# A planned kernel changes its PSUM layout: two double-bank and four single-bank tiles in place of four double-bank ones, scores chunk by chunk, and a planner that holds tiles back

## The chip, the cores and the metric

The kernel runs on one core of one Trainium2 chip. The metric is the device time of one execution in microseconds (us). Five engines take part, each working through its own list of instructions in order: PE (TensorE, matrix products and transposes; its weight loads are listed as PEld), DVE (VectorE), ACT (ScalarE), POOL (GpSimd) and SP, which issues nearly all DMAs. They wait for each other through semaphores.

## What is computed

A linear-attention recurrence (4 batches, 8 heads, 768 tokens, 48 values a head), whose output goes into a mixing block (384 channels):

```
state = 0                                        # per batch, head: D x D
for t in range(S):
    y[t] = r[t] @ (state + outer(u * k[t], v[t]))
    state = w[:, None] * state + outer(k[t], v[t])
x = y of all heads side by side                  # B, S, 384
theta = x @ w_theta
yr = w_tok_r @ (x * cos(theta));  yi = w_tok_i @ (x * sin(theta))
u = x + yr + yi
out = u + relu(u @ w_ch)
```

## The kernel before, in words

The 768 tokens of a batch are six chunks of 128, worked on as three pairs of chunks. There are so twelve pairs, and the names below are those of the steps and of the tiles that the profile prints.

For each batch, POOL scales r by powers of w (`Rw`, L491; on DVE in batch 0), PE transposes it in four groups (L472) and ACT copies the result out of PSUM (`RT`, L260). For each pair (`attention`):

- POOL scales k (`Kw`, L519), PE transposes it (L472, 8 transposes), ACT or DVE copies it out (`KT`, L260 or L262), and ACT casts v (`vb`, L260).
- PE makes the scores (16 matmuls on 64 rows, L543: two chunks, four pairs of heads, two heads each), DVE multiplies them by the mask (`mAT`, L549, two instructions). DVE makes `PD` (L554) and PE the diagonal term from it (L562), which ACT or DVE copies (`dg`) and POOL spreads over v (`yd`, L569).
- PE accumulates the outer products of k and v onto the state (L594, L586); DVE takes the state out after the first chunk (`Sb`, L601) and, scaled, after the second (`Sb`, L607).
- PE makes the pair's output from state and masked scores (L621, L626), DVE adds `yd` and has `x` (L633). PE transposes `x` (L472; copied out to `xT`) and multiplies by w_theta (L645); ACT takes sine and cosine (L649, L652), DVE and POOL the products `zr` (L655) and `zi` (L658).

When all three pairs of a batch have `zr` and `zi`, `mixing` makes the token product of each chunk in four parts of three matmuls that accumulate in one bank (L677), DVE adds `x` (`un`, L683), PE transposes (L472; `uT`), multiplies by w_ch (L694), DVE finishes (`fin`, L698) and SP stores (L702). The token weights come in twelve pieces that PE transposes first (L455, "W flips" here), from the same ring of ten `ld` buffers that k and v are loaded into.

Nothing of this order is written out by hand. Every step is a task with a cost, a priority, the keys that it reads and writes, and the PSUM space that it acquires and uses. `Plan.order` plays these tasks through with those costs: at each moment each engine takes the ready task of lowest priority number whose PSUM space is free, and the instructions are recorded in this order. On the chip each engine then runs its list in order, whatever the real durations are. The layer that records the instructions adds the semaphore waits; it keeps track of PSUM accesses by tile.

PSUM has eight banks. Before, they are four tiles of two banks. A task that needs one bank takes half a tile, so that two tasks that have nothing to do with each other can hold the two halves:

```
P = Plan(8)
banks = [ps.tile([C, 2, 512], F32, name=f"bank{i}") for i in range(4)]

def bank(tok):
    i = P.bank_of[tok]
    return banks[i // 2][:, i % 2]
```

Transposes, outer products, the diagonal term and the token product take one bank. The output of a pair, theta, the product with w_ch and a W flip take two. The scores of a pair take two times two: for each head of a pair of heads (`hi`) a double tile with both chunks.

Of the kernel before, what the change touches and what calls it, by code (L numbers as in the profile page):

```python
# [21 lines left out]
ENGINES = (PE, DVE, ACT, POOL, SP)  # L22


class Task:
    __slots__ = ("opts", "fn", "deps", "prio", "seq", "acq", "uses", "nwait", "users", "ready",
                 "start", "end", "mode", "lock", "eng", "name")


class Plan:  # L30
# [7 lines left out]
    def __init__(self, nbanks):  # L38
        self.tasks, self.writer, self.readers = [], {}, {}
        self.nbanks = nbanks  # L40
        self.bank_uses, self.bank_of, self.width = {}, {}, {}
# [30 lines left out]
    def pick_banks(self, acq, free, now):  # L72

        got = {}
        avail = [i for i in range(self.nbanks) if free[i] <= now]
        for tok in sorted(acq, key=lambda k: -self.width[k]):
            if self.width[tok] == 2:
                c = [i for i in avail if i % 2 == 0 and i + 1 in avail]
                if not c:
                    return None  # L80
                i = min(c, key=lambda i: max(free[i], free[i + 1]))
                avail.remove(i)
                avail.remove(i + 1)
            else:
                if not avail:
                    return None
                i = min(avail, key=lambda i: ((i ^ 1) in avail, free[i]))
                avail.remove(i)
            got[tok] = i
        return got  # L90

    def order(self):
        for t in self.tasks:
            t.users, t.nwait, t.ready = [], len(t.deps), 0.0
# [14 lines left out]
        free = [0.0] * self.nbanks  # L109
# [4 lines left out]
        while len(out) < n:  # L114
            for e in ENGINES:
                while free_at[e] <= now:
                    best, got = None, None
                    for t in waiting[e]:
                        if t.ready > now or (t.lock and port > now):
                            continue  # L120
                        if best is not None and (t.prio, t.seq) >= (best.prio, best.seq):
                            continue
                        if len(t.opts) > 1:
                            mine = now + t.opts[e][0]
                            if any(max(free_at[o], now) + t.opts[o][0] < mine
                                   for o in t.opts if o != e):
                                continue
                        g = {}
                        if t.acq:
                            g = self.pick_banks(t.acq, free, now)  # L130
                            if g is None:
                                continue
                        best, got = t, g
                    if best is None:
# [4 lines left out]
                    for tok, i in got.items():  # L139
                        self.bank_of[tok] = i  # L140
                        for j in range(self.width[tok]):
                            free[i + j] = INF
# [8 lines left out]
                    free_at[e] = now + ns  # L151
                    t.end = now + ns + lat
                    out.append(t)
                    for b in t.uses:
                        left[b] -= 1
                        freed[b] = max(freed.get(b, 0.0), t.end)
                        if left[b] == 0:
                            for j in range(self.width[b]):
                                free[self.bank_of[b] + j] = freed[b]
                    for x in t.users:  # L160
                        x.ready = max(x.ready, t.end)
# [4 lines left out]
            nxt += [t.ready for e in ENGINES for t in waiting[e] if t.ready > now]  # L166
# [59 lines left out]
def build(ctx, tc, nc, r, k, v, w, u, moe_w_theta, moe_w_tok_r, moe_w_tok_i, moe_w_ch, out):  # L226
# [12 lines left out]
    P = Plan(8)  # L239
    banks = [ps.tile([C, 2, 512], F32, name=f"bank{i}") for i in range(4)]  # L240

    def dbl(tok):
        return banks[P.bank_of[tok] // 2]

    def bank(tok):
        i = P.bank_of[tok]
        return banks[i // 2][:, i % 2]

    def bank16(tok):
        i = P.bank_of[tok]  # L250
        return banks[i // 2].bitcast(BF16)[:, i % 2]
# [57 lines left out]
    def setup():  # L309
# [6 lines left out]
        def fills(e):  # L316
# [7 lines left out]
        P.add({DVE: (600, 100)}, fills, wr=["ones", "wu", "pi2", "uw", "bmask"], prio=-200)  # L324
# [161 lines left out]
    def heads(b, base):  # L486

        rf, Rw, RT = r_fs[b % NR], Rws[0], RTs[b % 2]
        for hp in range(HP):
# [5 lines left out]
            opts = {POOL: pool_op(576, 2.1)}  # L495
# [9 lines left out]
    def attention(b, pr, base):  # L505
# [16 lines left out]
        opts = {POOL: pool_op(2 * HD)}  # L522
# [12 lines left out]
        tk = [("A", g, hi) for hi in range(2)]  # L535

        def scores(e):
            for c in range(2):
                cc = 2 * pr + c
                for hp in range(HP):  # L540
                    for hi in range(2):
                        q = slice(hi * Dp, (hi + 1) * Dp)
                        nc.tensor.matmul(dbl(tk[hi])[:, c, hp * C:(hp + 1) * C],  # L543
                                         KT[q, c, hp, :], RT[q, hp, cc * C:(cc + 1) * C],
                                         start=(hp == 0), stop=(hp == HP - 1))
        P.add({PE: pe_op(470)}, scores, rd=[kT] + rt_keys, acq=[(t, 2) for t in tk],
              prio=pb + 2, mode=1, name="scores")
        for hi in range(2):
            P.add({DVE: dve_op(8 * C)}, lambda e, hi=hi: nc.vector.tensor_mul(  # L549
                mAT[:, hi].rearrange("p a h t -> p (a h) t"),  # L550
                dbl(tk[hi]).rearrange("p a (h t) -> p (a h) t", h=HP), bc(mask01, 1, 2 * HP)),
                use=[tk[hi]], rd=["mask"], wr=[kM + (hi,)], prio=pb + 3, name="mask")
# [39 lines left out]
        def outer0(e):  # L592
# [8 lines left out]
        P.add({DVE: dve_op(HD)}, lambda e: nc.vector.tensor_mul(  # L601
            Sb_mid, bank(tS)[:, :HD].rearrange("p (h e) -> p h e", h=HP), bc(bmask, 1, HP)),
            use=[tS], rd=["bmask"], wr=[S_mid], prio=pb + 2.2, name="S")
# [9 lines left out]
        def outputs(e):  # L613
            for c in range(2):
# [10 lines left out]
                for h in range(H):  # L625
                    nc.tensor.matmul(dbl(ty)[:, c, h * D:(h + 1) * D], mAT[:, h % 2, c, h // 2, :],  # L626
# [131 lines left out]
```

## Time and profile before

| what | value |
|---|---|
| times of the runs shown | 235.33, 173.79 and 174.2 us, median 174.2 us |
| the profiled execution's own time | 173.87 us |
| its span, first to last instruction | 172.2 us |
| PE busy | 137.9 us (80%) |
| DVE busy | 113.2 us (66%) |
| POOL busy | 76.2 us (44%) |
| ACT busy | 71.6 us (42%) |

All durations come from the profiled execution, whose time is 1.7 us longer than its span. In rows of the timeline the columns are the start in us from the span's start, the duration in us, engine, line, operation, output and inputs by the program's names, and in brackets how long the engine stood idle just before, with what ended that. Rows of several instructions carry a count (x6). A busy PE is not PE at its peak, since matmuls are pipelined: one of 128x384 shows 326 ns, while 24 of them in a row take 3.90 us. In rows of the waits, the columns are the engine and line that waited, what it waited for, the total in us, the number of times and the longest.

### The profile page before, as it was taken

How to read it: one execution, taken by the hardware profiler on the slowest of the kernel's cores; microseconds unless marked ns; L12 is line 12 of the kernel's file. 1: busy time of each engine (PE TensorE's matmuls, PEld its weight loads, DVE VectorE, ACT ScalarE, POOL GpSimd, SP SyncE). 2: the span in 40 equal slices, each digit the busy share in tenths (PEclk: the TensorE clock that was granted, in tenths of full speed). 3: DMA queues.
4: the chain of work that ended last, by engine and by line, in shares of the span. 5: the costliest groups of instructions: out<-in, count | busy, mean ns of one | idle time of the engine just before them, and what ended most of it. 6: DMA issues, size and time to landing. Idle time of an engine off the chain costs nothing.

```text
span 172.2 us, 3640 instructions
## 1 busy us (share of the span) xinstructions
PE 137.9 (80%) x1491; PEld 96.1 (56%) x1491; DVE 113.2 (66%) x163; ACT 71.6 (42%) x102; POOL 76.2 (44%) x62
## 2 busy tenths in 40 slices
PE   3056699997969869968699999997899999699970
PEld 1046568786745646646485657566656665455530
DVE  6274976963418897476888668646799885344361
ACT  3966236775953425457633532556105213000000
POOL 6003328079941507999799791330333332100000
PEclk9999999999999999999969999999999999999995
DMA  5999999999993399799999900220020022020222
GB/s 164 239 240 163 169 372 373 392 372 157 177 159 53 92 325 152 136 197 195 344 161 157 168 12 20 75 91 0 4 91 4 0 93 89 6 91 0 91 91 91
DMA packets 59962, 25.00 MB, mean 145 GB/s; under 512 B 50473, under 2 KB 58410, under 8 KB 59946
## 3 DMA queue, kind: packets, MB, share of 16 engines
q1 hardware_dynamic: 59920, 24.78, 65.7%
q8 instruction: 11, 0.18, 0.5%
q14 instruction: 5, 0.04, 0.1%
q10 hardware_dynamic: 26, 0.00, 0.0%
HBM read 20.06 MB, written 4.72 MB: 144 GB/s over the span
## 4 chain that ended last, share of the span: by engine, by line
PE 53%; DVE 21%; ACT 11%; issue 7%; DMA 3%; POOL 3%; ACTq 1%; DVEq 0%; POOLq 0%
PE bank L677 22%; PE bank L472 8%; PE bank L694 7%; PE bank L645 6%; DVE mAT L549 5%; ACT RT L260 5%; DVE un L683 3%; DMA wu<-in_u_dram 3%; PE bank L626 2%; DVE fin L698 2%; DVE uT L262 2%; POOL zi L658 2%; PE bank L543 2%; DVE xT L262 2%; DVE Sb L601 2%
## 5 line engine op out<-in xcount | busy, mean ns | idle before, releaser
L677 PE MATMUL bank<-zi,WiT 128*128 128x384 bf16 x144 | 29.9, 326 | 3.7 <-DVE Sb L607 1.4
L569 POOL TENSOR_TENSOR yd<-dg,vb 128x768 bf16<-128x768 f32 x12 | 17.6, 1473 | 33.1 <-ACT dg L260 33.1
L677 PE MATMUL bank<-zr,WrT 128*128 128x384 bf16 x144 | 29.6, 326 | 2.9 <-ACT RT L260 1.4
L658 POOL TENSOR_TENSOR zi<-x,sin 128x768 bf16<-128x768 bf16 x12 | 19.9, 1657 | 25.0 <-ACT sin L649 25.0
L549 DVE TENSOR_TENSOR mAT<-bank,mask 128x1024 bf16<-128x1024 f32 x24 | 29.0, 1216 | 1.0 <-PE bank L543 1.0
L519 POOL TENSOR_TENSOR Kw<-ld,wpinv 128x768 bf16<-128x768 f32 x11 | 19.8, 1822 | 11.7 <-ACT RT L260 11.7
L683 DVE TENSOR_TENSOR un<-bank,x 128x384 bf16<-128x384 f32 x24 | 13.2, 555 | 16.4 <-PE bank L677 9.4
L677 PEld LDWEIGHTS <-WiT 128*128 128x128 bf16 x144 | 13.3, 97 | 11.7 <-issue 4.6
L677 PEld LDWEIGHTS <-WrT 128*128 128x128 bf16 x144 | 13.1, 97 | 11.1 <-issue 4.2
L649 ACT ACTIVATE sin<-bank 128x768 bf16<-128x768 f32 x12 | 9.7, 811 | 20.5 <-DVE fin L698 10.6
L260 ACT ACTIVATE RT<-bank 128x768 bf16<-128x768 bf16 x16 | 12.8, 815 | 9.4 <-PE bank L472 5.5
L491 POOL TENSOR_TENSOR Rw<-r_f,wpow 128x576 bf16<-128x576 f32 x12 | 16.6, 1409 | 0.0
L698 DVE SCALAR_TENSOR_TENSOR fin<-bank,un 128x768 f32<-128x768 f32 x12 | 11.5, 956 | 6.5 <-PE bank L694 6.4
L645 PE MATMUL bank<-Wth,xT 128*128 128x384 bf16 x72 | 14.7, 343 | 1.2 <-DVE xT L262 0.9
L694 PE MATMUL bank<-Wch,uT 128*128 128x384 bf16 x72 | 13.7, 327 | 1.4 <-DVE uT L262 1.4
L633 DVE TENSOR_TENSOR x<-bank,yd 128x768 bf16<-128x768 f32 x12 | 11.4, 951 | 2.5 <-PE bank L626 1.3
L655 DVE TENSOR_TENSOR zr<-bank,x 128x768 bf16<-128x768 f32 x12 | 11.4, 950 | 1.1 <-ACT bank L652 1.1
L472 PE MATMUL bank<-ident,Rw 128*128 128x128 bf16 x96 | 8.9, 241 | 3.4 <-ACT RT L260 1.9
L260 ACT ACTIVATE vb<-ld 128x768 bf16<-128x768 f32 x12 | 10.1, 840 | 3.5 <-DMA ld<-in_v_dram 3.4
L260 ACT ACTIVATE KT<-bank 128x1024 bf16<-128x1024 bf16 x7 | 7.2, 1023 | 9.5 <-PE bank L677 4.0
L626 PE MATMUL bank<-vb,mAT 128*128 128x48 bf16 x192 | 9.6, 189 | 1.7 <-DVE mAT L549 1.6
L652 ACT ACTIVATE bank<-bank,pi 128x768 f32<-128x768 f32 x12 | 10.5, 875 | 0.0
(76 smaller groups left out, 212.3 us busy)
## 6 DMA issues: line engine op xcount, KB each, us to landing
ld<-in_k_dram SPq DMA_DIRECT2D x24, 192.0 KB, 5.3
ld<-in_v_dram SPq DMA_DIRECT2D x24, 192.0 KB, 5.2
out_dram<-fin SPq DMA_DIRECT2D x12, 384.0 KB, 2.5
r_f<-in_r_dram SPq DMA_DIRECT2D x3, 1152.0 KB, 7.8
ld<-in_moe_w_tok_r_dram SPq DMA_DIRECT2D x6, 384.0 KB, 8.6
ld<-in_moe_w_tok_i_dram SPq DMA_DIRECT2D x6, 384.0 KB, 8.2
r_f<-in_r_dram SPq DMA_DIRECT2D x2, 576.0 KB, 4.6
ld<-in_moe_w_theta_dram SPq DMA_DIRECT2D x1, 384.0 KB, 5.0
```

Source lines behind the costliest of these rows:

```text
L260: nc.scalar.activation(dst, src, Act.Copy)
L472: nc.tensor.matmul(bank16(tok)[:, i * C:(i + 1) * C], s, ident, is_transpose=True, start=(i == 0), stop=(i == n - 1))
L491: eng_of[e].tensor_mul(Rw[:, :, 2 * hp:2 * hp + 2, :D].transpose([0, 2, 1, 3]), rf[:, 2 * hp:2 * hp + 2, :].rearrange("p h (n d) -> p h n ...
L519: eng_of[e].tensor_mul(Kw[:, :, :, :D].rearrange("p a h d -> p (a h) d"), Ls[ik][:, :, :, :D].rearrange("p a h d -> p (a h) d"), wpinv.rea ...
L549: P.add({DVE: dve_op(8 * C)}, lambda e, hi=hi: nc.vector.tensor_mul(mAT[:, hi].rearrange("p a h t -> p (a h) t"), dbl(tk[hi]).rearrange("p ...
L569: P.add({POOL: pool_op(2 * HD, 1.7)}, lambda e: nc.gpsimd.tensor_mul(yd.rearrange("p a (h d) -> p (a h) d", h=H), wide(dg, D), vb.rearrang ...
L645: nc.tensor.matmul(dbl(th)[:, t, :HD], xT[:, ND * t + dk, :], Wth[:, dk, :], start=(dk == 0), stop=(dk == ND - 1))
L658: P.add({POOL: pool_op(2 * HD, 1.9)}, lambda e: nc.gpsimd.tensor_mul(zi[:, 2 * pr:2 * pr + 2], x[:, 2 * pr:2 * pr + 2], sn), rd=xk + [("si ...
L677: nc.tensor.matmul(bank(tm)[:, :HD], WT[:, so, to * C:(to + 1) * C], z[:, so], start=(part == 0 and j == 0), stop=(part == 3 and j == 2))
L683: P.add({DVE: dve_op(HD)}, lambda e, tm=tm, t=t, to=to: nc.vector.tensor_add(un[:, t], bank(tm)[:, :HD], x[:, to]), use=[tm], rd=[("x", zj ...
L694: nc.tensor.matmul(dbl(tf)[:, t, :HD], uT[:, ND * t + dk, :], Wch[:, dk, :], start=(dk == 0), stop=(dk == ND - 1))
L698: P.add({DVE: dve_op(2 * HD)}, lambda e: nc.vector.scalar_tensor_tensor(fin, dbl(tf)[:, :, :HD], 0.0, un, op0=Alu.max, op1=Alu.add), use=[ ...
```

## The change

Three things are changed together.

PSUM becomes six tiles: two of two banks (slots 0 and 1) and four of one bank (slots 2 to 5). A task that needs one bank takes the smallest free tile that holds it, so a single-bank task may hold a double tile, but no two tasks share one.

The scores of a pair become two tasks, one for each chunk, each with 8 matmuls into one double tile (the two halves are now the two heads) and one mask instruction. `mAT` is turned round accordingly.

The planner changes in five points. A task that finds no tile free keeps the one that will be free first from tasks of higher priority number (`kept`). Readiness is counted for each engine, so that a task on the same engine as the one before it doesn't wait out the latency. PE costs count 1.6 times in the first 25 us (`cold`). POOL's costs for k and r are a little higher. And the state after the first chunk may be taken out by ACT too, in two copies of 64 partitions (the four `Sb` tiles are cleared once at the start, by four DVE fills).

```
+SLOTS = (2, 2, 1, 1, 1, 1)
...
+            c = [i for i in avail if self.slots[i] >= self.width[tok]]
+            if not c:
+                return None
+            i = min(c, key=lambda i: (self.slots[i], free[i]))
...
                             if g is None:
+                                c = [i for i in range(len(self.slots)) if i not in kept and
+                                     self.slots[i] >= max(self.width[k] for k in t.acq)]
+                                if c:
+                                    kept.add(min(c, key=lambda i: free[i]))
                                 continue
...
+                        if now < self.cold:
+                            ns *= 1.6
...
+                            x.ready[o] = max(x.ready[o], t.done if o == e else t.end)
...
-    P = Plan(8)
-    banks = [ps.tile([C, 2, 512], F32, name=f"bank{i}") for i in range(4)]
+    P = Plan(SLOTS)
+    banks = [ps.tile([C, n, 512], F32, name=f"bank{i}") for i, n in enumerate(SLOTS)]
...
+            for t in Sbs:
+                nc.vector.memset(t, 0.0)
...
-            opts = {POOL: pool_op(576, 2.1)}
+            opts = {POOL: pool_op(576, 2.15)}
...
-        opts = {POOL: pool_op(2 * HD)}
+        opts = {POOL: pool_op(2 * HD, 2.15)}
...
-        tk = [("A", g, hi) for hi in range(2)]
-
-        def scores(e):
-            for c in range(2):
-                cc = 2 * pr + c
+        for c in range(2):
+            tk, cc = ("A", g, c), 2 * pr + c
+
+            def scores(e, tk=tk, c=c, cc=cc):
...
-                        nc.tensor.matmul(dbl(tk[hi])[:, c, hp * C:(hp + 1) * C],
+                        nc.tensor.matmul(dbl(tk)[:, hi, hp * C:(hp + 1) * C],
...
-        P.add({PE: pe_op(470)}, scores, rd=[kT] + rt_keys, acq=[(t, 2) for t in tk],
-              prio=pb + 2, mode=1, name="scores")
...
+            P.add({PE: pe_op(235)}, scores, rd=[kT] + rt_keys, acq=[(tk, 2)],
+                  prio=pb + 2, mode=1, name="scores")
+            P.add({DVE: dve_op(8 * C)}, lambda e, tk=tk, c=c: nc.vector.tensor_mul(
+                mAT[:, c].rearrange("p a h t -> p (a h) t"),
+                dbl(tk).rearrange("p a (h t) -> p (a h) t", h=HP), bc(mask01, 1, 2 * HP)),
+                use=[tk], rd=["mask"], wr=[kM + (c,)], prio=pb + 3, name="mask")
...
-        P.add({DVE: dve_op(HD)}, lambda e: nc.vector.tensor_mul(
-            Sb_mid, bank(tS)[:, :HD].rearrange("p (h e) -> p h e", h=HP), bc(bmask, 1, HP)),
-            use=[tS], rd=["bmask"], wr=[S_mid], prio=pb + 2.2, name="S")
+        def mid(e):
+            src = bank(tS)[:, :HD].rearrange("p (h e) -> p h e", h=HP)
+            if e == DVE:
+                nc.vector.tensor_mul(Sb_mid, src, bc(bmask, 1, HP))
+            else:
+                for hi in range(2):
+                    q, f = slice(hi * Dp, (hi + 1) * Dp), slice(hi * D, (hi + 1) * D)
+                    copy(e, Sb_mid[q, :, f], src[q, :, f])
+        P.add({DVE: dve_op(HD), ACT: (490, 135)}, mid,
+              use=[tS], rd=["bmask", "Sb0"], wr=[S_mid], prio=pb + 2.2, name="S")
```

How this moves instructions is seen at three places. In the rows, a tile's number stands behind its name (`bank0` to `bank3` before, `bank0` to `bank5` after, followed by a running number). Weight loads and repeated rows are left out.

The first place is PE around the second pair of batch 1, between that pair's outer products (`Kw0`, the pair's scaled k) and the next pair's (`Kw1`). Before:

```order
L586 MATMUL bank3_64<-vb4_104,Kw0_96 128x96
L472 MATMUL bank0_61<-ident_66,Kw1_97 128x128
L677 MATMUL bank0_61<-zr0_126,WrT_142 128x384
L562 MATMUL bank3_64<-uw_82,PD0_109 128x2
L677 MATMUL bank0_61<-zi0_128,WiT_143 128x384
L594 MATMUL bank3_64<-Sb2_116,ident_66 128x384
```

After:

```order
L585 MATMUL bank4_65<-vb4_106,Kw0_98 128x96
L561 MATMUL bank2_63<-uw_84,PD0_111 128x2
L683 MATMUL bank3_64<-zr0_128,WrT_144 128x384
L473 MATMUL bank5_66<-ident_68,Kw1_99 128x128
L683 MATMUL bank3_64<-zi0_130,WiT_145 128x384
L651 MATMUL bank1_62<-Wth_142,xT1_135 128x384
L593 MATMUL bank2_63<-Sb2_118,ident_68 128x384
```

Before, the token product and the transposes of k stand in the two halves of `bank0`, and outer product and diagonal term in those of `bank3`. Now each of the four has a tile of its own.

The second place is PE at the end of batch 0's attention, from the third pair's output (L626; L632 after) to its theta (L645; L651 after, both from `xT0`) and the next W flips (L455; L456 after). Before:

```order
L626 MATMUL bank3_64<-vb2_102,mAT2_113 128x48
L455 MATMUL bank2_63<-ident_f_65,ld4_87 128x128 x6
L455 MATMUL bank0_61<-ident_f_65,ld5_88 128x128 x6
L455 MATMUL bank1_62<-ident_f_65,ld6_89 128x128 x6
L472 MATMUL bank2_63<-ident_66,x0_124 128x128
L472 MATMUL bank2_63<-ident_66,Rw0_95 128x128
L455 MATMUL bank3_64<-ident_f_65,ld7_90 128x128 x6
L645 MATMUL bank0_61<-Wth_140,xT0_132 128x384
L455 MATMUL bank1_62<-ident_f_65,ld8_91 128x128 x6
```

After:

```order
L632 MATMUL bank0_61<-vb2_104,mAT2_115 128x48
L473 MATMUL bank3_64<-ident_68,Rw0_97 128x128
L473 MATMUL bank2_63<-ident_68,x0_126 128x128
L456 MATMUL bank0_61<-ident_f_67,ld0_85 128x128 x6
L456 MATMUL bank1_62<-ident_f_67,ld1_86 128x128 x6
L473 MATMUL bank4_65<-ident_68,Rw0_97 128x128
L651 MATMUL bank0_61<-Wth_142,xT0_134 128x384
L456 MATMUL bank1_62<-ident_f_67,ld2_87 128x128 x6
L473 MATMUL bank5_66<-ident_68,Rw0_97 128x128
L456 MATMUL bank1_62<-ident_f_67,ld3_88 128x128 x6
```

Of the twelve W flips, nine stand ahead of this theta before (the four shown here and five earlier ones) and three behind it. After, three stand ahead of it (those from `ld9`, `ld0` and `ld1`) and nine behind. The flip that reads `ld3`, the buffer that the first k of batch 1 is then loaded into, stood ahead of the third pair's output and now stands behind its theta.

The third place is ACT, around the copies of k of the later batches, up to the next sine. Before:

```order
L260 ACTIVATE KT1_108<-bank1_62 128x1024
L260 ACTIVATE dg0_118<-bank1_62 128x16
L260 ACTIVATE KT0_107<-bank3_64 128x1024
L260 ACTIVATE xT0_132<-bank1_62 128x768
L260 ACTIVATE vb4_104<-ld6_89 128x768
L649 ACTIVATE sin0_130<-bank0_61 128x768
```

After:

```order
L259 ACTIVATE KT0_109<-bank5_66 128x1024
L259 ACTIVATE Sb3_119<-bank3_64 64x4x48 x2
L259 ACTIVATE vb4_106<-ld6_91 128x768
L259 ACTIVATE xT0_134<-bank5_66 128x768
L259 ACTIVATE Sb1_117<-bank2_63 64x4x48 x2
L259 ACTIVATE vb0_102<-ld8_93 128x768
L655 ACTIVATE sin0_132<-bank0_61 128x768
```

Two states that DVE took out before are now copied by ACT, ahead of the sine. Of the twelve states after a first chunk ACT takes seven. SP's list moves in one point: the load of r for batch 2 stands ahead of the first k of batch 1, and before it stood behind the first store. POOL scales r for batch 2 ahead of the first k of batch 1, and before it did so behind all three.

More of the change, by code (lines that the diff above doesn't have):

```diff
@@ L117, in order @@
                     best, got = None, None
[L118 to L121, printed above, removed]
+                    kept = set()
+                    for t in sorted(waiting[e], key=lambda t: (t.prio, t.seq)):
+                        if t.ready[e] > now or (t.lock and port > now):
                             continue
@@ L140, in order @@
                         self.bank_of[tok] = i
-                        for j in range(self.width[tok]):
-                            free[i + j] = INF
+                        free[i] = INF
                     ns, lat = t.opts[e]
```

59 lines of the change are left out of this document (21 added, 38 removed).

## Prediction

> **What bounds the kernel now.** I read the page first, then busy time by stage, then PE's waits stage by stage, then the timeline at the waits. The page's first lines:
>
> ```profile
> span 172.2 us, 3640 instructions
> PE 137.9 (80%) x1491; PEld 96.1 (56%) x1491; DVE 113.2 (66%) x163; ACT 71.6 (42%) x102; POOL 76.2 (44%) x62
> ```
>
> PE is the busiest and leaves 34.3 us idle. Busy time in five stretches: until the first transposes, batch 0's attention with the W flips, the steady part up to the last theta, the last batch's token product, and the last store. The columns are the length and then busy us (and instructions) of PE, PEld, DVE, ACT and POOL, the granted clock, and DMA:
>
> ```profile
> 0.00:8.80 8.80, 1.85 (x3) 0.70 (x4) 4.39 (x16) 6.15 (x12) 2.98 (x15) 1.00 0.95 201
> 8.80:51.00 42.20, 33.44 (x367) 26.90 (x368) 25.82 (x33) 26.00 (x37) 21.85 (x14) 1.00 1.19 259
> 51.00:143.24 92.24, 81.06 (x988) 56.38 (x986) 70.86 (x97) 37.83 (x53) 49.77 (x32) 0.98 0.54 112
> 143.24:167.60 24.36, 21.55 (x139) 12.13 (x137) 11.22 (x17) 1.58 (x2) 1.63 (x1) 1.00 0.18 65
> 167.60:172.20 4.60, 0.00 (x0) 0.00 (x0) 0.96 (x1) 0.00 (x0) 0.00 (x0) 0.59 0.24 85
> ```
>
> PE idles 7.0, 8.8, 11.2, 2.8 and 4.6 us. The first and the last stretch are loads, tables and a store, and the change leaves them as they are. The middle three hold 22.8 us that could go. In the steady part PE is busy 88% of the time, so that what its waits cost is nearly all paid. These are waits of PE, first in the front stretch, then in the steady part, then at the end:
>
> ```profile
> PE bank L472 <- ACT RT L260: 1.9, 2, 1.0
> PE bank L677 <- ACT RT L260: 1.8, 2, 1.4
> PE bank L472 <- DVE Sb L601: 0.4, 1, 0.4
> ...
> PE bank L677 <- DVE Sb L607: 1.4, 3, 0.6
> PE bank L677 <- ACT KT L260: 0.9, 1, 0.9
> PE bank L586 <- DVE xT L262: 0.7, 1, 0.7
> PE bank L677 <- DVE un L683: 0.6, 2, 0.3
> PE bank L472 <- ACT RT L260: 0.5, 1, 0.5
> PE bank L677 <- ACT RT L260: 0.3, 1, 0.3
> ...
> PE bank L677 <- DVE un L683: 1.3, 2, 1.2
> ```
>
> The token product (L677) reads neither the state `Sb` nor `KT` nor `RT`, and the outer products (L586) don't read `xT`. One of them in the timeline:
>
> ```profile
> 57.62 0.55 DVE L607 TENSOR_TENSOR Sb<-bank,wS 128x384 bf16<-128x384 f32 x1
> ...
> 58.22 0.65 PE L677 MATMUL bank<-zi,WiT 128*128 128x384 bf16 x3 [0.60 <-DVE Sb L607]
> ```
>
> This is a later part of an accumulation that had its bank long since, so it isn't waiting for space. What ties it to `Sb` is the tile: the state stands in one half of a double tile, the token product in the other, and the recording layer orders accesses by tile. Counted in the two built programs, 96 waits between PE, DVE and ACT are for an instruction that shares only the tile, not a bank and no data. After the change there is none.
>
> **The change part by part.** *The direct waits.* From the rows: front 1.9+1.8+0.4 = 4.1 us, steady part 1.4+0.9+0.7+0.6+0.5+0.3 = 4.4, end 1.3. All go, since a single-bank task has its tile alone.
>
> *The late copies.* The tie works the other way too. A copy out of PSUM waits for work in the other half, and PE then waits for the copy:
>
> ```profile
> 15.43 0.69 DVE L262 COPY KT<-bank 128x1024 bf16<-128x1024 bf16 x1 [3.43 <-ACT RT L260]
> ...
> 76.53 0.56 DVE L683 TENSOR_TENSOR un<-bank,x 128x384 bf16<-128x384 f32 x1 [0.53 <-ACT RT L260]
> 77.14 0.34 PE L472 MATMUL bank<-ident,un 128*128 128x128 bf16 x3 [1.33 <-DVE un L683]
> ...
> 81.52 0.56 DVE L262 COPY xT<-bank 128x768 bf16<-128x768 bf16 x1 [0.55 <-ACT RT L260]
> 82.14 1.15 PE L645 MATMUL bank<-Wth,xT 128*128 128x384 bf16 x6 [0.88 <-DVE xT L262]
> ...
> 84.60 0.56 DVE L607 TENSOR_TENSOR Sb<-bank,wS 128x384 bf16<-128x384 f32 x1 [0.86 <-PE bank L472]
> 85.21 0.34 PE L562 MATMUL bank<-uw,PD 128*128 128x2 bf16 x8 [0.65 <-DVE Sb L607]
> ```
>
> These add 1.33+0.88+0.65 = 2.8 us to the steady part (7.2 in all), and the copy of `KT` at 15.43 up to 1.3 in the front (5.4 in all). In the end stretch it stays at 1.3. What PE still waits for are true inputs, and they come earlier too.
>
> *The front.* Six W flips of about 0.85 us (row below) move from ahead of batch 0's last theta to behind it, 5.1 us. Theta can start up to 5.1 us earlier, if DVE's chain of masks and copies allows it, and 5.1 us more of flips follow before batch 1 starts. That is nothing net. Bounds: minus 5.1 (theta no earlier) to plus 5.4 (all tied waits gone). The four fills of `Sb` put a few tenths ahead of the tables. I take plus 1.0, just above the middle: batch 0 is a chain through DVE, whose work (70.86/9 = 7.9 us a pair in the steady part) hardly changes, but fewer copies for flips stand in it.
>
> ```profile
> 34.73 0.85 PE L455 MATMUL bank<-ident_f,ld 128*128 128x128 f32 x6
> 35.39 1.00 SPq L403 DMA_DIRECT2D ld<-in_k_dram  x2
> 41.33 1.15 PE L645 MATMUL bank<-Wth,xT 128*128 128x384 bf16 x6
> ld<-in_k_dram SPq DMA_DIRECT2D x24, 192.0 KB, 5.3
> ```
>
> *Two double tiles in place of four.* Every pair puts five things through them, with these holders after PE:
>
> ```profile
> L549 DVE TENSOR_TENSOR mAT<-bank,mask 128x1024 bf16<-128x1024 f32 x24 | 29.0, 1216 | 1.0 <-PE bank L543 1.0
> L649 ACT ACTIVATE sin<-bank 128x768 bf16<-128x768 f32 x12 | 9.7, 811 | 20.5 <-DVE fin L698 10.6 <-PE bank L645 9.9
> L652 ACT ACTIVATE bank<-bank,pi 128x768 f32<-128x768 f32 x12 | 10.5, 875 | 0.0
> L655 DVE TENSOR_TENSOR zr<-bank,x 128x768 bf16<-128x768 f32 x12 | 11.4, 950 | 1.1 <-ACT bank L652 1.1
> L633 DVE TENSOR_TENSOR x<-bank,yd 128x768 bf16<-128x768 f32 x12 | 11.4, 951 | 2.5 <-PE bank L626 1.3 <-POOL yd L569 1.2
> ```
>
> Two scores at 0.3+1.2, an output at about 0.9+0.95, theta at 1.15+0.81+0.88+0.95, and the w_ch product, as many matmuls as theta and then a DVE instruction of `x`'s size, at 1.15+0.95: 10.8 us a pair over two tiles, 5.4 us, where a pair now takes 92.2/9 = 10.2. Following the new order by hand with these durations from batch 1's first w_ch product to its third output, I find no place where PE would wait for a tile. The slack is (20.4-10.8)/5 = 1.9 us of queueing for each use. Cost 0 to 7 us; I take 1.0, near the lower end, since in that walk the tiles came free with tenths to spare, not microseconds.
>
> *Scores in two tasks.* The 12 additional groups issue the same matmuls. A group's own tail is what its row shows beyond the start of the next work:
>
> ```profile
> 83.22 0.62 PE L543 MATMUL bank<-RT,KT 64*128 64x128 bf16 x16
> 83.77 0.35 PE L586 MATMUL bank<-vb,Kw 128*128 128x96 bf16 x4
> ```
>
> 0.62-0.55 = 0.07 us, so 0 to 0.8 us; I take 0.5. The first mask can start half a group earlier, hidden behind DVE's queue.
>
> *Seven states on ACT.* DVE sheds 7x0.55 us (the `Sb` row above has this size). ACT takes two copies of 64 partitions for each, one of them between 0.18 us (the trace's 128x16 copy) and half of what 128x768 takes it, 0.41 us from the sine's row:
>
> ```profile
> L260 ACT ACTIVATE dg<-bank 128x16 f32<-128x16 f32 x9 | 1.6, 182 | 14.0 <-DVE Sb L601 5.0 <-PE bank L562 4.3 <-PE bank L677 3.6
> ```
>
> ACT is busy 37.83 of 92.24 us in the steady part, which hides it: cost 0. Without that cover it is 7x2x0.41-7x0.55 = 1.9 us at most; behind a state copy queue v's cast and the next sine, for which POOL's `zi` waits.
>
> *The sum.* Front 1.0, steady part 7.2-1.0-0.5 = 5.7, end 1.0 of 1.3: 7.7 us. The profiled execution took 173.87 us (span plus 1.7), so 166.2; the median of the runs shown stands 0.3 above it, so **166.5 us**.
>
> **The rivals.** *The double tiles become the bound (slower).* The place is the steady part. If DVE, in order and 77% busy there, makes each use hold its tile 2.3 us longer, a pair takes (10.8+5x2.3)/2 = 11.2 us, 1.0 more than now, over nine pairs 9 us: 173.9+9-2 (front and end) = 181 us. It decides from 1.9 us of delay on. For it: DVE's masks are 1.2 us, and two of anything ahead make 2.3. Against: the walk above, and that DVE loses its own waits.
>
> *The front gives it back.* The flip of `ld3` frees the buffer of batch 1's first k; the load was issued right behind it, at 35.39, and takes 5.3 us to land. It now follows theta. If theta stays at 41.33, the load is issued at 43.5 and k lands at 49, with POOL's scaling (behind four scalings of r for batch 2) still to come; the transposes of k that now end the front stretch, at 51, come some 4 us later, and 173.9-(5.7+1.0-4) = 171.2 us, no change. Against: if theta gains even 3 us, k lands at 46 and has 5 us left.
>
> *PE stays slow longer.* The same six matmuls of theta take twice as long early as later, at a granted clock of 1.00 in both:
>
> ```profile
> 25.25 2.10 PE L645 MATMUL bank<-Wth,xT 128*128 128x384 bf16 x6 [0.23 <-ACT xT L260]
> 33.55 1.14 PE L645 MATMUL bank<-Wth,xT 128*128 128x384 bf16 x6
> ```
>
> With flips moved out of batch 0's attention, PE is less busy there. Of the 16.1 us from this theta to the last one of the batch, at 41.33, nine flips took 7.7, which leaves at most 8.4 us of other work. If PE stays slow there, each us of it costs 2.10/1.14-1 = 0.84 more, 0 to 7 us, of which DVE's chain hides a part: 4 us, 171.2 again. The Trainium skill, "TensorE: Matmul & The Clock Gate", Part 1, has a rule for it: PE runs at half clock until it has been busy for a window of about 3.4 us, and falls back after an idle one. By that rule the time would be this rival's if PE fell idle that long. The longest of PE's front waits quoted above is 1.4 us, so the trace bears out the slow start but not the fall back.
>
> *All of it goes.* Every tied wait is gained and no tile is waited for: 5.4+7.2+1.3 = 13.9 us, 160.3 us in the runs' terms. For it: true inputs come earlier too. Against: an in-order PE usually finds the next wait.
>
> **How the numbers follow.** My forecast 0.60, all of it 0.14, the front 0.08, the slow clock 0.07, the tiles 0.11. A measurement of this kernel can tell about 2%, 3.5 us, from no change. Faster by more: 0.60+0.14 = 0.74; within: 0.15; slower: 0.11. The range for 8 in 10 reaches from 161.0, near the case where all goes, to 172.5, past the two that cancel; it leaves out the slower rival and half of the best case.
>
> **What would show it.** In the changed profile, no L683 token product waits for `RT`, `KT` or `Sb`, and no outer product for `xT`. PE's idle time in the steady part falls from 11.2 us to 4 to 6, while its busy time stays within 1 us of 137.9. What waits remain on PE are for masks, `xT`, `uT` and `un`. Batch 0's last theta starts near 37 and batch 1's first k transposes near 50. I am wrong if PE's tied waits are gone and its idle time stays, with waits for `mAT`, `zr` or `fin` at L543, L627 and L651 in their place, or if the tied waits were mere markers and PE's idle time was another's all along.

## The result and the profile after

| kernel | times of the runs | median | ratio to before, 95% interval |
|---|---|---|---|
| before | 173.79, 173.85, 174.2, 235.33 us | 174.02 us | 1 |
| after | 157.89, 158.26, 158.63, 159.55 us | 158.44 us | 0.912 [0.905, 0.918] |

The change gains 15.6 us, twice what was forecast. The 235.33 us is a disturbed run and isn't in the ratio; further down, medians are over undisturbed runs too. The profiled execution took 159.55 us, the longest of the four, so that the profiled executions differ by 14.3 us (173.87 and 159.55). The page's first lines:

```profile
span 157.8 us, 3653 instructions
PE 135.1 (86%) x1491; PEld 94.8 (60%) x1491; DVE 110.0 (70%) x158; ACT 76.3 (48%) x119; POOL 75.6 (48%) x61
```

The same stretches as in the prediction, without the last, which is 4.60 us in both (length, busy us of PE, PEld, DVE, ACT and POOL, granted clock, DMA):

```profile
0.00:8.80 8.80, 1.86 (x3) 0.70 (x4) 4.38 (x20) 6.12 (x12) 2.98 (x15) 1.00 0.94 201
8.80:51.00 42.20, 35.00 (x363) 27.51 (x364) 25.99 (x34) 26.43 (x39) 23.77 (x16) 0.92 1.17 269
51.00:131.00 80.00, 77.16 (x987) 53.89 (x985) 67.35 (x87) 42.15 (x68) 47.22 (x29) 1.00 0.66 124
131.00:153.20 22.20, 20.98 (x142) 12.69 (x140) 11.29 (x17) 1.58 (x2) 1.64 (x1) 1.00 0.20 72
```

Set beside the lines of before, each stretch splits into what PE idles less and what it is busy less:

| stretch | before | after | gain | of it PE idle | of it PE busy | predicted gain |
|---|---|---|---|---|---|---|
| front | 42.20 | 42.20 | 0.0 | 1.6 | -1.6 | 1.0 |
| steady part | 92.24 | 80.00 | 12.2 | 8.3 | 3.9 | 5.7 |
| end | 24.36 | 22.20 | 2.2 | 1.6 | 0.6 | 1.0 |

The sum is 14.4 us, the whole difference of the spans (172.2 and 157.8). PE's waits in the steady part of after, the complete answer:

```profile
PE bank L651 <- DVE xT L261: 1.4, 1, 1.4
PE bank L543 <- DVE fin L704: 0.5, 1, 0.5
PE bank L543 <- DVE zr L661: 0.5, 1, 0.5
PE bank L561 <- DVE PD L553: 0.4, 2, 0.3
```

Theta waits for its own `xT`, the diagonal term for its own `PD`, and the scores twice for a double tile (`fin` and `zr` read one). Every wait has a true reason. The token product (now L683) waits for nothing.

Two things stand out already. PE is 3.9 us less busy in the steady part, with as many matmuls (988 and 987); the prediction had no term for that. And the front, where 5.4 us of tied waits were counted, gained nothing.

### The profile page after: what moved, and what is told of

It is laid out like the page before. It is cut to its first block, busy times and chain, and to the rows that moved or that the text cites. A ratio compares the mean times of both kernels' runs of the same rounds, so it can differ in the third digit from the quotient of the medians.

```text
span 157.8 us, 3653 instructions
## 1 busy us (share of the span) xinstructions
PE 135.1 (86%) x1491; PEld 94.8 (60%) x1491; DVE 110.0 (70%) x158; ACT 76.3 (48%) x119; POOL 75.6 (48%) x61
## 4 chain that ended last, share of the span: by engine, by line
PE 49%; DMA 14%; DVE 11%; POOL 9%; SPq 9%; issue 3%; ACT 2%; ACTq 0%; POOLq 0%; DVEq 0%
PE bank L683 22%; DMA r_f<-in_r_dram 11%; SPq L404 8%; PE bank L473 7%; PE bank L700 6%; POOL Rw L492 5%; PE bank L456 4%; DMA ld<-in_k_dram 4%; PE bank L651 3%; POOL Kw L520 3%; DVE zr L661 2%; PE bank L543 2%; DVE PD L553 2%; DVE mAT L548 1%; DVE un L689 1%
## 5 line engine op out<-in xcount | busy, mean ns | idle before, releaser
L683 PE MATMUL bank<-zi,WiT 128*128 128x384 bf16 x144 | 29.7, 326 | 0.0
L683 PE MATMUL bank<-zr,WrT 128*128 128x384 bf16 x144 | 29.2, 326 | 0.0
L520 POOL TENSOR_TENSOR Kw<-ld,wpinv 128x768 bf16<-128x768 f32 x10 | 18.6, 1861 | 19.8 <-DMA ld<-in_k_dram 16.8
L664 POOL TENSOR_TENSOR zi<-x,sin 128x768 bf16<-128x768 bf16 x12 | 20.6, 1715 | 15.2 <-ACT sin L655 15.2
L651 PE MATMUL bank<-Wth,xT 128*128 128x384 bf16 x72 | 15.4, 357 | 2.8 <-DVE xT L261 1.4
L683 PEld LDWEIGHTS <-WiT 128*128 128x128 bf16 x144 | 12.9, 98 | 7.1
L683 PEld LDWEIGHTS <-WrT 128*128 128x128 bf16 x144 | 12.8, 97 | 7.0
L259 ACT ACTIVATE vb<-ld 128x768 bf16<-128x768 f32 x12 | 10.1, 845 | 11.8 <-DMA ld<-in_v_dram 11.3
L259 ACT ACTIVATE RT<-bank 128x768 bf16<-128x768 bf16 x16 | 12.0, 816 | 4.7 <-PE bank L473 4.6
L651 PEld LDWEIGHTS <-xT 128*128 128x128 bf16 x72 | 7.3, 104 | 8.2 <-issue 2.7
L543 PE MATMUL bank<-RT,KT 64*128 64x128 bf16 x192 | 9.8, 229 | 2.1 <-ACT KT L259 0.6
L473 PE MATMUL bank<-ident,Kw 128*128 128x128 bf16 x96 | 8.4, 241 | 1.9 <-POOL Kw L520 1.7
```

The costliest lines, as they stand in the source:

```text
L259: nc.scalar.activation(dst, src, Act.Copy)
L473: nc.tensor.matmul(bank16(tok)[:, i * C:(i + 1) * C], s, ident, is_transpose=True, start=(i == 0), stop=(i == n - 1))
L520: eng_of[e].tensor_mul(Kw[:, :, :, :D].rearrange("p a h d -> p (a h) d"), Ls[ik][:, :, :, :D].rearrange("p a h d -> p (a h) d"), wpinv.rea ...
L651: nc.tensor.matmul(dbl(th)[:, t, :HD], xT[:, ND * t + dk, :], Wth[:, dk, :], start=(dk == 0), stop=(dk == ND - 1))
L664: P.add({POOL: pool_op(2 * HD, 1.9)}, lambda e: nc.gpsimd.tensor_mul(zi[:, 2 * pr:2 * pr + 2], x[:, 2 * pr:2 * pr + 2], sn), rd=xk + [("si ...
L683: nc.tensor.matmul(bank(tm)[:, :HD], WT[:, so, to * C:(to + 1) * C], z[:, so], start=(part == 0 and j == 0), stop=(part == 3 and j == 2))
```

## Experiment 1: the ties put back, and nothing else

The changed kernel's plan is kept task by task, and each engine's list is the same. The four single slots stand in the same banks, but as halves of two double tiles, so that the recording layer ties them again:

```
-    banks = [ps.tile([C, n, 512], F32, name=f"bank{i}") for i, n in enumerate(SLOTS)]
+    tiles = [ps.tile([C, 2, 512], F32, name=f"bank{i}") for i in range(4)]
+    place = [(0, 0), (1, 0), (2, 0), (2, 1), (3, 0), (3, 1)]
...
-        return banks[P.bank_of[tok]][:, 0]
+        i, h = place[P.bank_of[tok]]
+        return tiles[i][:, h]
```

> The changed kernel's order, engine by engine and instruction by instruction, but single slots 2 and 3 as the halves of one double tile, 4 and 5 as those of another: 95 waits between PE, DVE and ACT come back that share only a tile (before had 109 by this count, with PE, DVE and ACT together in both directions). Theory T1, the ties are the whole gain: 170 to 174 us, PE idle in the steady part back at 9 to 11 us. Rival T2, the planner's new order is the gain and ties cost little: 158 to 161 us. Rival T3, half and half: 164 to 167 us.

In a second kernel only slots 2 and 3 are tied (`place` ends in `(2, 0), (2, 1), (3, 0), (4, 0)`, with tiles 3 and 4 of one bank):

> As the run before, but only slots 2 and 3 are tied; 4 and 5 stay single tiles: 46 of the 95 waits come back. T1: about half of the loss of the run before, 164 to 167 us. T2: 158 to 160 us.

Measured: 176.6 us with all ties (ratio to before 1.016 [1.012, 1.021]), 169.7 us with half of them (0.978 [0.971, 0.984]). Both lie above the ranges of T1 (170 to 174 and 164 to 167 us): the theory has the cause right and its size too small. (The count of before is 96, as the prediction says, not 109; 109 is that of experiment 2's first kernel.) The ties alone cost this order 18.2 us, more than the whole gain; with ties the new order is no better than the old one (1.6% slower). Half of the ties cost 11.3 us, more than half. The page of the kernel with all ties:

```profile
span 174.5 us, 3662 instructions
PE 138.0 (79%) x1491; PEld 95.2 (55%) x1491; DVE 113.0 (65%) x158; ACT 76.3 (44%) x119; POOL 75.1 (43%) x61
```

Against after, PE idles 36.5 - 22.7 = 13.8 us more and is busy 2.9 us longer: 16.7 us, the difference of the spans. The stretches of this kernel, from the first transposes of batch 1's k on:

```profile
52.60:146.10 93.50, 81.91 (x986) 55.58 (x985) 70.44 (x87) 42.37 (x68) 46.54 (x29) 0.98 0.61 106
146.10:169.94 23.84, 21.16 (x141) 12.65 (x141) 11.30 (x17) 1.58 (x2) 1.64 (x1) 1.00 0.18 67
```

The steady part is 93.5 us long, about as before the change (92.2). How a tie works there, in the timeline of PE and then of DVE:

```profile
109.83 0.65 PE L686 MATMUL bank<-zi,WiT 128*128 128x384 bf16 x3
110.31 0.65 PE L686 MATMUL bank<-zr,WrT 128*128 128x384 bf16 x3
111.62 0.65 PE L686 MATMUL bank<-zr,WrT 128*128 128x384 bf16 x3 [0.65 <-DVE un L692]
112.10 0.50 PE L476 MATMUL bank<-ident,un 128*128 128x128 bf16 x6
```

```profile
111.00 0.56 DVE L692 TENSOR_TENSOR un<-bank,x 128x384 bf16<-128x384 f32 x1 [0.99 <-PE bank L686]
```

`un` reads the half that the matmuls of the first row filled, until 110.48 (109.83 + 0.65). It starts only at 111.00, when PE's next three, which fill the other half, are done at 110.96: about 0.5 of DVE's 0.99 us of idling is the tie. PE's three matmuls after that go into this other half again and wait for `un`. Two engines that could work side by side take turns. The same matmuls of PE, the last six in one piece, and the same `un`, in after:

```profile
100.02 0.65 PE L683 MATMUL bank<-zi,WiT 128*128 128x384 bf16 x3
100.51 1.14 PE L683 MATMUL bank<-zr,WrT 128*128 128x384 bf16 x6
101.48 0.50 PE L473 MATMUL bank<-ident,un 128*128 128x128 bf16 x6
```

```profile
100.71 0.56 DVE L689 TENSOR_TENSOR un<-bank,x 128x384 bf16<-128x384 f32 x1 [0.51 <-PE bank L683]
```

`un` runs while PE multiplies, and its wait is for the bank that it reads (filled at 100.67).

These rows also show where the busy time went. From the first of the six matmuls to the start of the next work are 0.97 us in after (100.51 to 101.48) and 1.79 us in the tied kernel (110.31 to 112.10), 0.82 more. The profile shows 0.65 us of that as idle. The other 0.17 stands in busy: in a stream a matmul overlaps the next one by this much, which is why the rows' durations (0.65 for three) are longer than 0.97/2, and over a stop nothing overlaps. Compared instruction by instruction (each adds the time by which it ends later than the one before it): of the 19 stops over 0.15 us behind the front that only the tied kernel has, 15 make the first matmul 160 ns longer (323 in place of 163 for 128x384, 217 in place of 56 for a transpose) and 4 make it 54 ns longer; the mean is 0.14 us. The Trainium skill, "TensorE: Matmul & The Clock Gate", Part 2 ("Single matmul latency" and the gap formula behind it), states this: alone and at full clock a matmul of N columns takes (398+N)/2.4 ns, in a row N/2.4+2.5; the two differ by some 163 ns whatever N is. The trace agrees at the 15 stops.

Over the whole steady part the tied kernel's PE stops 27 times, after's 5 times (counted in the trace). 22 x 0.14 = 3.1 us of the 4.8 us by which PE is busier there (81.91 and 77.16). For the rest there is one stretch of 3.4 us at half clock in the tied kernel, from 73.2 us on, which can hold at most 1.7 us.

On the ties themselves the Trainium skill's "PSUM — Partial Sum Buffer", in its section on bank collisions, asks for semaphores by bank and quadrant of partitions. A tile of two banks guards more than that. The banks were the same with and without ties here, so the 18.2 us are for waits that this rule doesn't ask for.

## Experiment 2: layout and planner apart

First the four double tiles of before, with the rest of the change (scores chunk by chunk, states on ACT too, readiness by engine, `cold`, `kept`, POOL's costs):

> The kernel before's four double-bank tiles and its choice of halves, with everything else of the change: scores chunk by chunk, states on ACT too, readiness by engine, the slower first 25 us, tiles held back. 109 waits tied by a tile alone, as many as before. T1: 171 to 175 us, as before. T2: 159 to 163 us. T3: 165 to 168 us.

Then the new tiles with the planner of before (`cold`, `kept`, readiness, POOL's costs and states on DVE as they were). The scores have to go chunk by chunk here, because the old ones need both double tiles of the new layout at once and leave none for an output that is under way:

> Only the two double-bank and four single-bank tiles, with the scores chunk by chunk (with two double tiles the old two-tile scores can't be placed); the planner's other rules and its prices as before, states on DVE alone. No tied waits. T1: 157 to 161 us. T2: 168 to 173 us. T3: 163 to 166 us.

| | planner as before | planner as after |
|---|---|---|
| four double tiles, ties | 173.7 us (before) | 180.45 us, 1.040 [1.035, 1.045] |
| two double and four single, no ties | 160.8 us, 0.926 [0.918, 0.933] | 158.4 us, 0.912 [0.905, 0.918] |

The layout with chunk-wise scores is worth 12.9 us under the old planner. The planner's points and the states on ACT are worth some 2.4 us without ties (the intervals touch) and lose 6.7 us with them. The theory that the new order is the gain has fallen. The upper row isn't as clean as the lower: its right kernel makes the scores chunk by chunk, its left one doesn't, so that the 6.7 us hold that too. Why the new order loses with ties is argued, not shown: the planner plays the halves of a tile as independent, so what it packs more densely is tied more often (109 tied waits in place of 96).

## Experiment 3: the change's other parts, one at a time

Each kernel is after with one thing taken back, and a new plan. States on DVE alone (`{DVE: dve_op(HD), ACT: (490, 135)}` without ACT):

> The changed kernel with the states on DVE alone (the planner's order follows). Theory, as predicted: ACT's share is hidden and DVE's relief too, 157.5 to 160.5 us. Rival: with the ties gone DVE (67.35 of 80.00 us busy in the steady part) is the next limit, and its 7 states of 0.55 us come back: 161.5 to 163 us.

The planner's slower first 25 us removed (`cold = 0.0`):

> The changed kernel with the planner's slower first 25 us removed: batch 0's attention is then planned without W flips between its matmuls, and eight W flips follow its last theta. Theory: the front stretch is set by batch 0's chain through DVE and by loads, and the place of the flips is worth nothing net: 156 to 160 us, first transposes of batch 1's k at 48 to 52 us. Rival, PE stays slow longer where no flips fill it: front 3 to 5 us longer, 161.5 to 164 us. Rival, the slower first stretch in the plan is what the front lost: front at 47 to 48 as in the run with the layout alone, 154.5 to 156 us.

Readiness for all engines with the full latency (`t.end` in place of `t.done if o == e else t.end`, and the choice between two engines without `t.ready[o]`):

> The changed kernel with the input of a task counted as ready with the full latency on its own engine too, as before. Theory: the order shifts by tenths, nothing in the sum: 157.5 to 160.5 us. Rival: the difference between the run with the layout alone (161.3 us) and the change (158.4 us) lies here: 160.5 to 163 us.

And after itself once more, as a measure of what such differences mean:

> The changed kernel once more, beside the others of this call: 157.5 to 159.5 us.

| kernel | median | ratio to before |
|---|---|---|
| after, first and again (the latter of two executions) | 158.4 and 158.9 us | 0.912 [0.905, 0.918], 0.917 [0.910, 0.923] |
| states on DVE alone | 160.8 us | 0.930 [0.925, 0.935] |
| without `cold` | 157.3 us | 0.910 [0.905, 0.914] |
| readiness as before | 160.3 us | 0.926 [0.921, 0.932] |

`cold` is worth nothing that can be told. Without either of the other two the kernel is 0.9 to 1.5% slower, at or just over the upper end of what was expected if they did nothing, and under the 2% that the prediction takes as the least that can be told. DVE's relief isn't the reason: with the states on DVE the steady part is as short as in after:

```profile
50.00:129.60 79.60, 76.26 (x976) 52.71 (x974) 69.03 (x93) 38.69 (x56) 44.89 (x28) 1.00 0.68 125
```

Each of the three kernels also orders PE's tasks differently (48 to 107 of 254 moved), so that a part's own share can't be told from the luck of an order. `kept` has no share in the result: without it the plan comes out the same in order and tiles.

## Experiment 4: how many double tiles

Three double and two single tiles, `SLOTS = (2, 2, 2, 1, 1)`:

> Three double-bank and two single-bank tiles in the change's place. Theory: two double tiles are enough (PE waited 2.8 us for one in all), and two tiles fewer are available: same or slower, 158 to 162 us. Rival, the double tiles are the next bound: 155 to 157 us.

One double and six single ones, `SLOTS = (2, 1, 1, 1, 1, 1, 1)`:

> One double-bank tile and six single ones in the change's place. By the prediction's price of 10.8 us of double tiles a pair, one tile would set the steady part: nine pairs by 10.8 us and its queueing, 97 to 110 us in place of the 80 us, and 175 to 195 us in all. Rival, the walk overstates how long a tile is held, and one of them nearly does: 160 to 168 us.

Measured: 158.8 us with three (0.918 [0.915, 0.922]), 225.0 us with one (1.300 [1.293, 1.307]). A third double tile is worth nothing, as expected. One alone costs some 66 us, far more than worked out. Page and waits of that kernel:

```profile
span 225.2 us, 3651 instructions
...
PE 157.3 (70%) x1491; PEld 107.8 (48%) x1491; DVE 114.1 (51%) x164; ACT 75.8 (34%) x113; POOL 75.1 (33%) x61
```

```profile
PE bank L543 <- DVE zr L661: 14.1, 6, 3.0
PE bank L627 <- DVE mAT L548: 7.9, 6, 1.3
```

The scores wait for the tile that theta holds until `zr`, and the output for the masks: every holder's chain of PE, ACT and DVE now stands on PE's path. The nine pairs of the steady part take 127.8 us (66.70 to 194.50), 14.2 us a pair where the time of one tile times the uses gave 10.8. That sum left out, probably, that with one tile the next holder's instructions also start only after the last one's end, and that PE gets slower; of this below.

## Experiment 5: a kernel that is faster than both

With the ties gone PE is busy for 86% of the span. Of its work the twelve W flips are avoidable: they transpose float32, 0.85 us each. Here the pieces are cast to bfloat16 first, into a buffer `lc`, and flipped as bfloat16 in a single-bank tile:

```
+                P.add({ACT: act_op(6 * C, False), DVE: dve_op(6 * C)},
+                      lambda e, i=i, m=m: copy(e, lcs[m], flat(i)[:, :S]),
+                      rd=L2(i) + ["tables done"], wr=[("lc", m)], prio=prio + to, name="Wcast")
+                flips(dst[:, :, to * C:(to + 1) * C],
+                      [lcs[m][:, o * C:(o + 1) * C] for o in range(NCH)], tok, prio + to,
+                      [("lc", m)], [(key, to)], "Wflip",
+                      {ACT: act_op(6 * C), DVE: dve_op(6 * C, 2.0)})
```

With casts on ACT alone, two `lc` and one buffer fewer for v:

> The changed kernel with the token weights cast to bfloat16 on ACT before their flips (the values were rounded to bfloat16 after the flip), two buffers for the casts and one fewer for v: a flip takes 6 x 0.056 us in place of 0.85, uses a single-bank tile, and the load buffer is free after the cast. With the ties gone PE is busy 86% of the span, so its work is the price: 12 x 0.5 = 6 us of PE busy go. Theory, PE is the bound: 153 to 156 us. Rival, the front is set by batch 0's chain and the loads, and PE's relief falls on idle time: 157 to 160 us.

With casts on ACT or DVE, one `lc`, as in the diff:

> As the run before, with the casts on ACT or DVE as the planner finds them free, one buffer for the casts and all five for v. Theory: 153 to 156 us; if DVE's part stands in batch 0's chain, 1 to 2 us over the run before.

Measured: 157.7 us (0.909 [0.905, 0.914]) and 156.1 us (0.901 [0.897, 0.906]), the second under after's repeat beside it (158.9 us, 0.917 [0.910, 0.923]); against after's first measurement the intervals touch. The theory that PE is the bound (153 to 156 us) misses the first, which lies in the rival's range, and nearly holds for the second. PE is busy 129.8 us in it, 5.3 less than in after. Of that 2.3 to 2.8 us come through in the medians, and 4.0 in the spans of the profiled executions (157.8 and 153.8). Its front and steady part, with one of its loads:

```profile
9.10:47.00 37.90, 29.15 (x354) 21.45 (x355) 29.08 (x41) 27.46 (x39) 19.16 (x12) 0.86 1.20 271
47.00:124.90 77.90, 75.58 (x979) 53.31 (x977) 68.33 (x87) 45.84 (x74) 52.29 (x33) 1.00 0.68 140
```

```profile
36.43 1.01 SPq L406 DMA_DIRECT2D ld<-in_k_dram  x2
```

The front ends at 47.0 in place of 51.0. Batch 1's first k load is issued at 36.43. In after it goes out later, behind the load of W_ch on SP's queue, and POOL scales r four times ahead of that k:

```profile
38.82 2.07 SPq L404 DMA_DIRECT2D ld<-in_moe_w_ch_dram  x2
42.68 1.01 SPq L404 DMA_DIRECT2D ld<-in_k_dram  x2
```

```profile
42.81 5.53 POOL L492 TENSOR_TENSOR Rw<-r_f,wpow 128x576 bf16<-128x576 f32 x4
48.29 1.82 POOL L520 TENSOR_TENSOR Kw<-ld,wpinv 128x768 bf16<-128x768 f32 x1
```

The time doesn't hang on that load, though. In after PE goes from the token product into the transposes of k without a stop:

```profile
50.54 0.65 PE L683 MATMUL bank<-zi,WiT 128*128 128x384 bf16 x3
51.03 0.61 PE L473 MATMUL bank<-ident,Kw 128*128 128x128 bf16 x8
```

And with three double tiles (experiment 4) the same load goes out at 36.43 too and the transposes start 6 us earlier than in after, with no gain in time (158.8 us):

```profile
36.43 1.08 SPq L404 DMA_DIRECT2D ld<-in_k_dram  x2
```

```profile
45.00 0.61 PE L473 MATMUL bank<-ident,Kw 128*128 128x128 bf16 x8
```

What the kernel with casts has less of is PE's work: 29.15 us in its front in place of 35.00, and behind the front 98.8 us, about as after's 98.2. That PE's work sets the time here is the reading that fits both kernels; since each has an order of its own, it is not shown by itself.

## Why the prediction was wrong, step by step

**That ties bind PE** was right: experiment 1 undoes the gain with them alone, and no rival with a slower end came.

**The steady part, 7.2 us of tied waits, is the step that failed, by its size.** It measured 12.2 us with the costs already inside, where 5.7 was put. The prediction took a wait's price to be the idle time in its row. In the steady part PE stopped 26 times before and 5 times after (counted in the trace), and each stop also costs what experiment 1 showed, 0.14 us in the mean, which the profile books as busy: 21 x 0.14 = 2.9 of the 3.9 us by which PE is less busy. For the remaining 1.0 us there is the granted clock, 0.98 before and 1.00 after. Before had one stretch of 3.4 us at half clock there, after has none; that can hold at most 1.7 us, and its share is argued:

```profile
86.50:89.90 3.40, 3.40 (x52) 3.00 (x51) 2.72 (x4) 1.21 (x3) 3.40 (x3) 0.50 1.09 151
```

So the sign "busy time within 1 us of 137.9" failed: it is 135.1. The evidence was there: the groups of three that follow a wait show 0.65 us, while 24 of the same matmuls take 3.90 us in a row, 0.49 for three. The prediction used such a tail once, for the scores, and not where it had a dozen waits in hand.

**The idle time left** was put at 4 to 6 us and is 2.8 (11.2 before). The count of 7.2 us held only waits that end with a tied one; that the true inputs come earlier as well was named and not priced. Measured are 8.3 us with the 1.0 us of the two waits for a tile already taken off, so 9.3 in all, 2.1 more than counted.

**The costs.** Two double tiles at 1.0 us: the two waits for a tile in the steady part are 0.5 + 0.5, and experiment 4 finds that two suffice and one doesn't. The rival in which they become the bound needs one tile fewer. Scores in two tasks at 0.5 us can't be separated, since the layout needs them. Seven states on ACT at nothing holds for the steady part (79.6 and 80.0 us).

**The end, 1.0 us,** measured 2.2: 1.6 of idle and 0.6 of busy. All of the tied 1.3 us seems to have come through, and a stop was priced too low here too.

**The front, plus 1.0 us,** measured nothing. Theta 3 starts at 39.1, where 37 was expected, and k's transposes at 51.0, where 50 was. Two rivals came in part. Batch 1's k load went out at 42.68, near the 43.5 of the rival in which the front gives the gain back. Its price of 4 us more was wrong: before had issued this load at 35.39 and its transposes stood at 50.8 all the same, so that the load had slack.

The other rival is that PE stays slow longer. More of PE's work did fall into slow time, but in another way. The traces' record of the clock begins at 28.5 us in before and at 22.1 in after; ahead of it the profile shows 1.00, though the matmuls are slow. (In before the eight transposes of a k take 1.01 us at 18.16 and 0.61 at 29.20; in after eight score matmuls take 0.61 at 20.12 and 0.40 at 22.66.) So PE was fast 6 us sooner in after, and then it fell back twice, for 3.4 us each. The three thetas of batch 0 in after, the stretches around the two falls, and the slow beginnings of before and of after:

```profile
25.40 1.98 PE L651 MATMUL bank<-Wth,xT 128*128 128x384 bf16 x6 [0.63 <-DVE mAT L548]
...
32.46 2.08 PE L651 MATMUL bank<-Wth,xT 128*128 128x384 bf16 x6 [0.71 <-DVE mAT L548]
...
39.08 1.14 PE L651 MATMUL bank<-Wth,xT 128*128 128x384 bf16 x6
```

```profile
22.10:25.50 3.40, 2.05 (x31) 1.29 (x30) 3.40 (x6) 2.36 (x5) 1.03 (x1) 1.00 1.01 388
25.50:28.90 3.40, 3.38 (x38) 2.33 (x37) 1.76 (x3) 2.69 (x3) 0.97 (x1) 0.51 1.04 384
28.90:32.40 3.50, 1.72 (x20) 1.27 (x21) 3.42 (x4) 0.72 (x2) 2.10 (x2) 0.99 1.07 373
32.40:35.80 3.40, 3.34 (x32) 2.33 (x32) 0.00 (x1) 1.42 (x3) 2.60 (x2) 0.50 1.04 395
```

```profile
8.80:28.50 19.70, 14.44 (x145) 11.43 (x146) 13.85 (x18) 10.01 (x16) 6.77 (x5) 1.00 1.28 257
```

```profile
8.80:22.10 13.30, 10.62 (x125) 8.77 (x125) 11.21 (x17) 6.21 (x11) 3.68 (x3) 1.00 1.40 194
```

The second theta takes 2.08 us, where before had 1.14. In slow time PE is busy 10.62 + 3.38 + 3.34 = 17.3 us in after and 14.4 in before. If such work takes 2.08/1.14 as long, the 2.9 us more hold some 1.3 us of lost time (an estimate), of the 1.6 by which PE is busier in the front (35.00 and 33.44). That eats the 1.6 us of idle that it gained. The rival was right in kind and had 4 us for it. The prediction said that the trace of before bears out the slow start and not a fall back; but the stretch from 86.50 to 89.90 above is one.

**The case that all of it goes** (160.3 us, a chance of 0.14) came nearest; 158.4 us lies 1.9 us under it. It had no term for the busy time of the stops, 2.9 us.

What stays open: how the last 2.4 us divide among the planner's points, why the old layout loses 6.7 us with them, and what the ties cost in the order of before, which no run has without them.

## What to carry to other kernels

If waits are tracked by tile, the tile has to be as small as what is waited for: banks that hold unrelated work should be tiles of their own, even where that leaves fewer wide ones. Price a stop of PE as the idle time in the row plus the overlap that is lost (0.14 us in the mean here), and count stops as well as idle time. A planner's rules pay only if it knows every tie that the program will have: the same rules went with a gain of 2.4 us without ties and a loss of 6.7 us with them (there with the scores chunk by chunk as well).

## What the hardware showed unexpectedly

The granted clock falls to half in stretches of 3.4 us or a multiple of it. In after this happens twice in the front (rows above), and never in the denser steady part. What comes just ahead is in the same rows: 3.4 us in which PE is busy for 2.05, and 3.5 us with 1.72. The record of the clock goes by stretches of 3.4 us. In the fourteen traces, divided like this, 59 of the stretches at full clock have PE busy for at most 62%, by the profile's count, and 41 of these are followed by half clock. The other 483 have it busy for more, and none of these is followed by half clock. This is a count and no experiment; why 18 quiet stretches aren't followed stays open.

With one double tile the clock is 0.81 over the whole run, and PE is busy 157.3 us with the same number of matmuls as after's 135.1: stops and the lower clock both add to that; their shares weren't separated. With four double tiles and the new planner, where PE idles 40.4 us of 178.3, it is 1.00. There the idle time is spread out: up to the last matmuls only two stretches have PE busy for at most 62%, and neither is followed by half clock.

The Trainium skill, "TensorE: Matmul & The Clock Gate", Part 1, has the clock fall back after an idle window of about 3.4 us; no wait of PE in after's front is that long (the longest, for POOL's `Kw`, is 1.7 us). The length agrees; but here a window that is idle for only 40% (2.05 us busy of 3.40) came ahead of a fall.
